# A new order of work for a fused sigmoid-attention and token-mixing kernel on one Trainium2 core

## The chip, the cores and the metric

The kernel runs on one core of one Trainium2 chip. The time is the device time of one execution in microseconds (us); before the change it is 184.6 us, the median of three runs (183.64 to 184.81). The core has five engines with queues of their own, each of which works off its list strictly in order: PE (TensorE, matmuls), DVE (VectorE), ACT (ScalarE), POOL (GpSimd) and SP (SyncE, which here only issues DMAs).

## The reference

Per batch (8) and head (12) the reference computes a sigmoid attention over 448 positions with 64 dimensions, then a token-mixing layer on the joined heads (768 wide):

```python
scores = scale * np.matmul(q, k.transpose(0, 1, 3, 2)) - np.log(S)
attn = 1.0 / (1.0 + np.exp(-scores))
x = np.matmul(attn, v)                  # heads joined: x is (8, 448, 768)
wq = x @ w_q ; wk = x @ w_k             # 64 wide
W_tok = scale * einsum('bsd,btd->bst', wq, wk)
mixed = einsum('bst,btd->bsd', W_tok, x)
out = np.maximum(mixed, 0.0) @ w_out    # float32, (8, 448, 768)
```

## The kernel before, in words

The kernel takes four heads of one batch at a time; such a set is called a *group* here (in the code `quads`), and there are 8 x 3 = 24 of them, numbered 0 to 23. Three groups make a batch (`u`). Matmuls run in bf16 with sums in PSUM, which is used as eight banks, single (`bank1`) or in pairs (`bank2`).

For each group there are these steps, with the line of the instruction in brackets:

- SP loads q, k and v as float32 into a ring of six buffers `ld` (L190, L198). A buffer is free for the sixth load after it when its cast is done.
- The casts to bf16 run on POOL, or on DVE where the table `ORDER` has a dot ahead of the name (L222 for plain casts, L212 for casts that interleave pairs of elements).
- q and k are brought into transposed form in one of four ways, given by letters of the table `PLAN` and recorded in `KIND`: `q`/`k`, by 28 matmuls each on quadrants (64 x 64) of the array (L124), with one copy by DVE for both (L301); `a`/`b`, by 7 matmuls each on the whole array (128 x 128), with one copy each (L280); `c`/`d`, exchanged by POOL (function `arrange`: L167 once, L170 and L173 twice each) and then transposed in blocks by DVE (L272 twice); `r`/`s`/`z`, in quadrants by DVE alone (L265 twice, L252 four times).
- Letter `S` (seven in a group): one slice of scores, four matmuls on quadrants (L121, tiles `banks<-qk`), then the sigmoid on ACT over 896 elements per partition (L332). `T` is an `S` whose sigmoid is put off, so that the next one covers both slices in one instruction of 1792 elements.
- `P` (seven in a group): attention times v, four matmuls on quadrants into one pair of banks; after the seventh the sum is copied to `xt` (L356 on DVE; small `p` on ACT).
- `x`: transposes `xt` to `xn` with 28 matmuls on quadrants into a pair of banks; `X` does it with 7 matmuls on the whole array into a single bank (L124, copy L385).

Once per batch: `W` (six times, x times w_q and w_k), `N` and `U` (tmp, evacuated at L463), `M` (three times, the mixing with its relu, L470), and `O` (the product with w_out, copied at L604 or L651 and stored). POOL copies one half of `wq` for it (L438).

Nothing of this order is left to a scheduler. `PLAN` is a string of letters worked off from left to right, and every step appends its instructions to the lists of the engines. `BANKS` gives the banks in the order of request (digits are pairs, letters single banks). `ORDER` is the order of loads and casts; POOL's casts are appended as soon as their buffers allow it (`pump`), DVE's where `PLAN` has a `1`. `D` issues the next output store. `HELD` and `BEHIND` make some stores and loads wait until a numbered matmul is done.

Of the kernel before, what the change touches and what calls it, by code (L numbers as in the profile page):

```python
# [17 lines left out]
def kernel(  # L18
# [29 lines left out]
    def pool(name, bufs, **kw):  # L48
# [15 lines left out]
    pairs = [banks[:, 2 * n : 2 * n + 2] for n in range(4)]  # L64
    pairs16 = [banks16[:, 2 * n : 2 * n + 2] for n in range(4)]
    BANKS = (
        "abcd0123200233111020302312031203101031021g2012020120h1g21320"
        "132123103103213012302g01h20h1g2031a32102312g12h1201321gh0210"
        "12h01210321g201321g2h01gh201g20132cd302c302302131e301230ef31"
        "0ef3102102c302d320d320123cd20gh120g102310g102hg102312gh10210"  # L70
        "ef130210ef1302120120320312321031021021321a310320321320120123"
        "020210320120c3210210312"
    )
    given = list("".join(BANKS))
    held = set()
# [54 lines left out]
    def xt(u, j):  # L130
# [5 lines left out]


    PLAN = (
        "SSFKESSES1EEqESDD1DESjPPppSpDpPDSSSqS1kSpPPSqSpSkSDPPSPSxSxr"
        "sSWwDDDDSSwzDPpSPppSpPSrSwSwWsSPpXSPNpSpPPSUSqSzMSSkpSpPpSMS"  # L140
        "ppPSSxSxMScPpSdPSpppSSPwWwrWSSXWDWSSosOSNPpPSpppzPSSOOSxSrPP"
        "ppSUSsppzPSoSOSoSoSppMpSPPPPSSWOWWWScSdxWODSMDWSOSxCOSMppScP"
        "DppSPPDSodDoSpxPDPDSCPrPSpDSPOOSNSsSOoDzOOSUSXcSPdpPSSpPPSPo"
        "OWSMSwowWMSSOwWCScpppSxpdpSpPSOoMSPPcDSPPpSpSPOoNSSSdDOoDOOp"
        "xDSPpPxSPpPDSuwcWwdSSMWOoSMSDwwOOSDxpPSPrPSmPpPDooNDSDSosoOz"
        "oSDDSxOOSUDpSDPPPDSPpcDSPoDODSSSodOoOSPMpSPPPSPPSwWwoScMSdOw"
        "wSSWOONSPMPcpSPPPPSSOodXSOSxoSoxSOppSpcUPSPpPSoOSdSxOOSPPPmp"
        "pPSPoSoMmOSOLScllLSLLSDodODSONxOPSpcpdpDPSPSPoOSoSOSOoSUSoSO"
        "SpPPpp1SoSOpSPOSOyppPMpPpplMlmlxlLlxOoONooUoOMmooOmooOoOOOOO"
        "oOOOOooOo"  # L150
    )
    PLAN = "".join(PLAN)
    KIND = ["a"] + [t for t in PLAN if t in "qacr"]
# [364 lines left out]

    opened = []
    stores, o_tiles = [], [0]  # L520
    HELD = {(5, 1, 1): 3040, (5, 2, 0): 3168, (5, 2, 1): 3168}

    def flush(n=None):

# [45 lines left out]
    def out_pair(act, tail):  # L570
# [128 lines left out]
    for _ in range(31):  # L699
# [1 line left out]


    ORDER = (
# [5 lines left out]
    )  # L709
    BEHIND = {("q", 23): (2280, 2280), ("v", 23): (2816, 2530)}  # L710
    BY = {"s": [], "v": []}
    for x in ORDER.split():
        if x[0] == ".":
# [10 lines left out]
    def pump_loads():  # L724
        while len(loaded) < len(ORDER):
            nm, n = ORDER[len(loaded)]
            if len(ring) >= 6 and ring[-6] not in cast:
                break
            emit, m = BEHIND.get((nm, n), (0, 0))
            if emit >= len(products):  # L730
# [204 lines left out]
```

## Time and profile before

| | |
|---|---|
| median of three runs | 184.6 us (183.64 to 184.81) |
| the profiled execution | 184.71 us |
| span from its first to its last instruction | 182.8 us |
| granted TensorE clock, mean | 0.994 |
| busy: PE, DVE, ACT, POOL | 170.4, 134.3, 159.4, 116.8 us |
| DMA moved, mean | 48.51 MB, 265 GB/s |

The profile lists what each engine did in one execution. "Busy" is time in which at least one of its instructions was under way; the instructions of PE and ACT overlap their successors, so the distance from start to start says more of their pace than the duration. Timeline rows give start and duration in us, the engine, the line, the operation, the tiles it writes and reads (out<-in), the shape and the count, and in brackets how long the engine stood idle ahead of it and who ended that. A shape such as `64*64` ahead of a matmul's operands is the part of the array that it uses.

### The profile page before, as it was taken

To read this page: it belongs to the slowest core of one execution; us is meant where nothing else is said; L and a number is where in the kernel's file an instruction comes from. 1 tells how busy PE (TensorE), PEld (TensorE's weight loads), DVE (VectorE), ACT (ScalarE), POOL (GpSimd) and SP (SyncE) were. 2 spreads that over 40 slices of the span, in tenths; PEclk is the share of its full clock that TensorE was granted. 3 is DMA by queue.
4 is the path that set the end of the run, shared out by engine and by line. 5 is a ranking of instruction groups with operands and counts; after the bars stand their busy time and mean duration, and the time that the engine had idled before them with its cause. 6 is when DMAs were issued, how large, how long until landed. Compare 5 with 4: busy or idle time off the path is not lost.

```text
span 182.8 us, 8404 instructions
## 1 busy us (share of the span) xinstructions
PE 170.4 (93%) x3617; PEld 112.8 (62%) x3618; DVE 134.3 (73%) x205; ACT 159.4 (87%) x207; POOL 116.8 (64%) x156
## 2 busy tenths in 40 slices
PE   7887789899999999999999999999999999999980
PEld 7644435545564555565556556556788798899960
DVE  2545699988998898988858887689786885694220
ACT  4699999999999999999998999899989979966230
POOL 1336886999589999699999927999999500000000
PEclk9999999999999999999999999999999999999997
DMA  5999999969999677999999999997589343433775
GB/s 174 371 382 274 329 382 398 364 212 279 351 402 331 219 295 207 353 285 349 396 232 327 349 307 292 359 359 250 193 255 252 106 96 87 95 90 93 176 181 164
DMA packets 24261, 48.51 MB, mean 265 GB/s; under 512 B 3872, under 2 KB 16416, under 8 KB 24224
## 3 DMA queue, kind: packets, MB, share of 16 engines
q1 hardware_dynamic: 24000, 47.69, 79.4%
q8 instruction: 28, 0.46, 1.0%
q10 hardware_dynamic: 224, 0.30, 0.7%
q14 instruction: 9, 0.07, 0.1%
HBM read 35.78 MB, written 11.01 MB: 256 GB/s over the span
## 4 chain that ended last, share of the span: by engine, by line
PE 76%; ACT 12%; DMA 3%; POOL 3%; issue 2%; DVE 1%; POOLq 0%; ACTq 0%
PE banks L121 72%; ACT at L332 12%; PE banks L124 4%; DMA ld<-in_v_dram 3%; POOL v L222 1%; POOL qk L212 1%; POOL qk L173 1%; POOL wout L755 0%; DVE xn L385 0%; ACT qk L806 0%; DVE ld L558 0%; ACT ld L558 0%; DVE zeros L691 0%; DVE zeros L690 0%; POOLq L222 0%
## 5 line engine op out<-in xcount | busy, mean ns | idle before, releaser
L332 ACT ACTIVATE at<-banks 128x896 bf16<-128x896 f32 x168 | 141.1, 943 | 5.4 <-PE banks L121 4.8
L121 PE MATMUL banks<-wout,mx 64*64 64x384 bf16 (+2 forms) x816 | 65.4, 324 | 0.0
L121 PE MATMUL banks<-qk 64*64 64x448 bf16 x672 | 60.7, 360 | 3.8 <-ACT at L332 3.0
L212 POOL CAST qk<-ld 128x896 bf16<-128x896 f32 x38 | 44.7, 1191 | 8.2 <-issue 5.6
L121 PEld LDWEIGHTS <-mx 64*64 64x64 bf16 (+2 forms) x816 | 39.2, 105 | 16.2 <-issue 6.0
L121 PE MATMUL banks<-at,v 64*64 64x448 bf16 x672 | 46.5, 350 | 0.8 <-ACT at L332 0.4
L121 PEld LDWEIGHTS <-qk 64*64 64x64 bf16 x672 | 26.5, 105 | 24.8 <-issue 17.8
L356 DVE CAST xt<-banks 128x896 bf16<-128x896 f32 x23 | 25.0, 1086 | 7.6 <-PE banks L121 5.7
L121 PEld LDWEIGHTS <-v 64*64 64x64 bf16 x672 | 22.9, 106 | 6.8 <-issue 1.7
L470 DVE TENSOR_SCALAR mx<-banks 128x896 bf16<-128x896 f32 (+1 forms) x21 | 19.9, 956 | 4.9 <-PE banks L121 4.2
L222 POOL CAST v<-ld 128x896 bf16<-128x896 f32 x22 | 20.3, 930 | 2.9 <-DMA ld<-in_v_dram 2.7
L272 DVE STREAM_TRANSPOSE qk<-qk 128x448 f32<-128x448 f32 x26 | 16.0, 630 | 0.1
L385 DVE COPY xn<-banks 128x896 bf16<-128x896 bf16 x21 | 13.1, 624 | 3.6 <-PE banks L124 2.6
L252 DVE STREAM_TRANSPOSE qk<-qk 32x448 f32<-32x448 f32 x24 | 15.3, 636 | 0.6
L170 POOL COPY qk<-qk 32x448 uint32<-32x448 uint32 x26 | 14.4, 554 | 1.6
L173 POOL COPY qk<-swap 32x448 uint32<-32x448 uint32 x26 | 14.4, 554 | 1.5
L121 PE MATMUL banks<-xt,wqk 64*64 64x448 bf16 (+1 forms) x84 | 13.8, 353 | 0.2 <-ACT at L332 0.2
L651 DVE COPY o<-banks 128x384 f32<-128x384 f32 x17 | 9.4, 554 | 3.4 <-PE banks L121 3.0
L124 PEld LDWEIGHTS <-xt 64*64 64x64 bf16 (+1 forms) x588 | 9.8, 108 | 3.0 <-issue 1.5
L124 PE MATMUL banks<-ident,xt 64*64 64x64 bf16 (+1 forms) x588 | 10.4, 194 | 0.2
L121 PE MATMUL banks<-wqk,tmp 64*64 64x448 bf16 (+3 forms) x72 | 8.5, 291 | 0.0
L121 PE MATMUL banks<-wq,tmp 64*64 64x448 bf16 (+2 forms) x72 | 8.4, 292 | 0.0
(67 smaller groups left out, 135.3 us busy)
## 6 DMA issues: line engine op xcount, KB each, us to landing
ld<-in_q_dram SPq DMA_DIRECT2D x24, 448.0 KB, 6.2
ld<-in_v_dram SPq DMA_DIRECT2D x24, 448.0 KB, 5.9
ld<-in_k_dram SPq DMA_DIRECT2D x23, 448.0 KB, 5.9
out_dram<-o SPq DMA_DIRECT2D x38, 192.0 KB, 4.7
out_dram<-ld SPq DMA_DIRECT2D x14, 192.0 KB, 2.8
ld<-in_moe_w_out_dram SPq DMA_DIRECT2D x6, 384.0 KB, 4.6
wout<-wout SPq DMA_DIRECT2D x6, 192.0 KB, 6.0
out_dram<-o SPq DMA_DIRECT2D x4, 96.0 KB, 1.9
```

The costliest lines, as they stand in the source:

```text
L121: products.append(nc.tensor.matmul(*args, **kw))
L124: products.append(nc.tensor.transpose(*args, **kw))
L170: eng.tensor_copy(out=w[lo, 1], in_=w[hi, 0])
L173: eng.tensor_copy(out=w[hi, 0], in_=z[lo])
L212: COPY[e](out=f[:, :, "qk".index(nm)].rearrange("p e i d y -> p e y i d"), in_=ld.pop((nm, n)).rearrange("p (y i e d) -> p e y i d", y=2, ...
L222: COPY[e](out=t16.rearrange("p i b d -> p b i d"), in_=ld.pop((nm, n)).rearrange("p b (i d) -> p b i d", i=NI),)
L252: nc.vector.transpose(out=qk[n][other : other + 32, h].rearrange("p t i n -> p (t i n)").bitcast(F32), in_=w[own : own + 32, 1 - h],)
L272: nc.vector.transpose(out=qk[n][:, t].rearrange("p t i n -> p (t i n)").bitcast(F32), in_=w)
L332: nc.scalar.activation(dst, src, ACTF.Sigmoid, bias=attn_bias, scale=attn_scale)
L356: COPY[eng](out=xt(u, j), in_=ps)
L385: COPY[eng](out=xn, in_=ps)
L470: nc.vector.tensor_scalar(dst, ps, moe_scale, 0.0, ALU.mult, ALU.max)
```

## The change

The three tables are replaced; no function changes. `PLAN`, `BANKS` and `ORDER` are new as a whole, and `HELD` and `BEHIND` are empty, so that no load and no store waits for a numbered matmul.

```diff
     PLAN = (
-        "SSFKESSES1EEqESDD1DESjPPppSpDpPDSSSqS1kSpPPSqSpSkSDPPSPSxSxr"
+        "SSFKESSESEEDDEqSkDSSEpSpPPppSPSPPDS1qkS1ppSpSapSbSPTSSDrXSxS"
...
-    HELD = {(5, 1, 1): 3040, (5, 2, 0): 3168, (5, 2, 1): 3168}
+    HELD = {}
...
     ORDER = (
-        ".q1 k1 .v0 .k2 q2 v1 q3 k3 q4 w0 k4 v2 k5 q5 v3 q6 k6 v4 k7 w5 "
-        "q7 v5 w3 q8 w1 k8 w2 w4 w6 v6 v7 q9 k9 k10 v8 q10 q11 v9 v10 "
...
+        "q1 k1 v0 q2 v1 k2 .q3 q4 .k3 k4 w0 v2 q5 k5 q6 v3 q7 k6 v4 k7 v5 "
+        "w6 k8 w5 q8 w1 w3 w4 v6 w2 v7 q9 k9 v9 v10 .q10 k10 .v8 k11 q11 "
...
-    BEHIND = {("q", 23): (2280, 2280), ("v", 23): (2816, 2530)}
+    BEHIND = {}
```

Counted over both programs, the work itself is the same but for the following. Two groups change from 28 matmuls per operand on quadrants to 7 on the whole array (groups 3 and 6), and so do two transposes of `xt`: 6 x 21 = 126 matmuls fewer. Groups 9, 12 and 17 change from DVE's quadrants to POOL's exchange: 16 groups are exchanged now and were 13, three go in quadrants and were six. DVE makes 13 casts instead of 4: seven more at L212, two more at L222. Four sigmoids become two of double length. A few copies out of PSUM change between ACT and DVE (L604: two more on DVE; L385, L463, L651 and L470: one each).

The first place is POOL's list about group 9, whose casts are those into `qk_1133` before and `qk_1017` now; group 10 is `qk_1275` before and `qk_1230` now, and `wq_99` belongs to batch 1. Before:

```order
L212 CAST qk_1133<-ld_103 128x2x2x224
L212 CAST qk_1133<-ld_104 128x2x2x224
L438 COPY wq_99<-wqk_97 64x448
L212 CAST qk_1275<-ld_105 128x2x2x224
L222 CAST v_1278<-ld_100 128x2x7x64
L212 CAST qk_1275<-ld_101 128x2x2x224
L167 COPY swap<-qk_1275 128x448
L170 COPY qk_1275<-qk_1275 32x448 x2
L173 COPY qk_1275<-swap 32x448 x2
```

And now:

```order
L212 CAST qk_1017<-ld_103 128x2x2x224
L212 CAST qk_1017<-ld_104 128x2x2x224
L167 COPY swap<-qk_1017 128x448
L170 COPY qk_1017<-qk_1017 32x448 x2
L173 COPY qk_1017<-swap 32x448 x2
L438 COPY wq_99<-wqk_97 64x448
L222 CAST v_1296<-ld_105 128x2x7x64
L222 CAST v_1299<-ld_100 128x2x7x64
L212 CAST qk_1230<-ld_102 128x2x2x224
L167 COPY swap<-qk_1230 128x448
L170 COPY qk_1230<-qk_1230 32x448 x2
L173 COPY qk_1230<-swap 32x448 x2
```

Group 9 now has an exchange on POOL between its casts and its transposes, two casts of v stand ahead of group 10, and one of group 10's two casts is gone from POOL.

The second place is the same one in DVE's list. Before, from group 9's transposes on (`qk_1133`), to those of group 10 (`qk_1275`):

```order
L265 STREAM_TRANSPOSE qk<-qk_1133 128x448 x2
L463 CAST tmp<-banks 128x384
L252 STREAM_TRANSPOSE qk<-qk_1133 32x448 x4
L356 CAST xt_91<-banks 128x2x7x64
L651 COPY o<-banks 128x384
L470 TENSOR_SCALAR mx<-banks 128x2x448
L356 CAST xt_92<-banks 128x2x7x64
L272 STREAM_TRANSPOSE qk<-qk_1275 128x448 x2
```

And now, with group 9 as `qk_1017` and group 10 as `qk_1230`:

```order
L272 STREAM_TRANSPOSE qk<-qk_1017 128x448
L212 CAST qk_1230<-ld_101 128x2x2x224
L463 CAST tmp<-banks 128x384
L356 CAST xt_91<-banks 128x2x7x64
L272 STREAM_TRANSPOSE qk<-qk_1017 128x448
L222 CAST v_1294<-ld_103 128x2x7x64
L651 COPY o<-banks 128x384 x2
L470 TENSOR_SCALAR mx<-banks 128x2x448
L356 CAST xt_92<-banks 128x2x7x64
L272 STREAM_TRANSPOSE qk<-qk_1230 128x448 x2
```

Six transposes of group 9 have become two, with a cast of group 10's q and the evacuations of `tmp` and `xt` between them.

More of the change, by code (lines that the diff above doesn't have):

```diff
@@ L66 @@
     BANKS = (
[L67 to L72, printed above, removed]
+        "abcd2300122011333230123201203103c0d3013e012g0120201h2013e123"
+        "102g1h02130130213b21302g01h20h1g2031a32102312g102h012301gh02"
+        "1012h01210321h201321gh201gh201320132cd302c302302131e031203e0"
+        "f13ef1032102dc032032d032102cdg02h120g102302g012hg021302gh102"
+        "10ef130213fe13021201023203123120310210213213a103203213201201"
+        "23020120320c2d03110213212"
     )
```

22 lines of the change are left out of this document (11 added, 11 removed), and 6 rows, old and new, of the table ORDER.

## The prediction

> **What bounds the kernel now.** I read the page's busy line and chain first, then busy time by stage, then the engines' rows in order of time.
>
> ```profile
> PE 170.4 (93%) x3617; PEld 112.8 (62%) x3618; DVE 134.3 (73%) x205; ACT 159.4 (87%) x207; POOL 116.8 (64%) x156
> PE 76%; ACT 12%; DMA 3%; POOL 3%; issue 2%; DVE 1%; POOLq 0%; ACTq 0%
> ...
> core 0: us, PE busy (x) PEld busy (x) DVE busy (x) ACT busy (x) POOL busy (x), PEclk, DMA share, GB/s
> 0.00:6.70 6.70, 5.28 (x49) 4.72 (x49) 2.32 (x8) 2.48 (x4) 1.73 (x9) 1.00 0.72 227
> 6.70:52.90 46.20, 40.42 (x942) 22.53 (x943) 36.91 (x54) 45.84 (x57) 33.69 (x39) 1.00 0.96 338
> 52.90:130.00 77.10, 77.10 (x1314) 43.91 (x1306) 64.92 (x97) 73.99 (x98) 67.87 (x89) 1.00 0.90 306
> 130.00:159.30 29.30, 29.30 (x834) 25.14 (x830) 20.77 (x29) 27.78 (x35) 13.53 (x20) 1.00 0.57 156
> 159.30:177.60 18.30, 18.28 (x505) 16.45 (x497) 9.02 (x18) 8.99 (x17) 0.00 (x0) 1.00 0.52 128
> 177.60:182.80 5.20, 0.00 (x0) 0.00 (x0) 0.36 (x1) 0.32 (x1) 0.00 (x0) 0.80 0.62 171
> ```
>
> The stages are cut where the bound changes. From 6.7 to 52.9 us ACT is busy 45.84 of 46.20 us, all with sigmoids (56 end in it), while PE has 5.8 us without any matmul. From 52.9 to 177.6 us PE is never idle. ACT still has 73.99 of 77.10 us there, POOL 67.87, and DMA 0.90 of its engines. So ACT sets the first stage, PE the rest, with ACT and POOL close behind; the last 5.2 us are the last copies and stores, which the change leaves as they are.
>
> A busy PE still loses time. The distances from start to start show where:
>
> ```profile
> 80.55 1.14 PE L121 MATMUL banks<-wout,mx 128*128 128x384 bf16 x6
> 81.52 0.35 PE L121 MATMUL banks<-xt,wqk 128*128 128x448 bf16 x1
> ...
> 86.92 0.37 PE L121 MATMUL banks<-qk 64*64 64x448 bf16 x4
> 87.11 0.56 PE L121 MATMUL banks<-at,v 64*64 64x448 bf16 x8
> 87.49 0.38 PE L121 MATMUL banks<-qk 64*64 64x448 bf16 x4
> 87.80 1.15 PE L121 MATMUL banks<-wout,mx 128*128 128x384 bf16 x6
> 88.88 0.38 PE L121 MATMUL banks<-wqk,tmp 64*64 64x448 bf16 x2
> ```
>
> Four score matmuls followed by others on quadrants take 0.19 us (86.92 to 87.11); the same four followed by whole-array ones take 0.31 (87.49 to 87.80). Six output matmuls followed by whole-array ones take 0.97, followed by quadrants 1.08. So going from one tile size to the other costs PE about 0.12 us, either way. Counted along the program's PE list, the tile size changes 84 times before and 86 times now: some 10 us of each.
>
> **The change part by part.** First PE, in the whole-array transposes:
>
> ```profile
> 77.44 0.38 PE L121 MATMUL banks<-qk 64*64 64x448 bf16 x4
> 77.75 0.56 PE L124 MATMUL banks<-ident,xt 128*128 128x128 bf16 x7
> 78.25 0.38 PE L121 MATMUL banks<-qk 64*64 64x448 bf16 x4
> ...
> 130.33 0.39 PE L124 MATMUL banks<-ident,xt 64*64 64x64 bf16 x28
> 130.55 0.66 PE L121 MATMUL banks<-wout,mx 64*64 64x384 bf16 x12
> ```
>
> 28 transposes on quadrants take 0.22 us; 7 on the whole array, between scores, take 0.50, and the scores ahead of them 0.31 instead of 0.19. So the 126 matmuls fewer are no gain: 0.50 - 0.12 for the way back = 0.38, less 0.22, is 0.16 us more for each of six, 1.0 us, beside the changes of tile size. But all six lie ahead of the 56th sigmoid (two groups early, and four `X` there against two before), where ACT sets the pace: I cost them at nothing. Their cover is the 5.8 us of idle PE there; without it they cost 1.0 us.
>
> The changes of tile size move the same way. Ahead of the 56th sigmoid there are now 29 of them (21 before), behind it 57 (63 before). Values, W, M and O ahead of that sigmoid are the same in number. So PE's work behind 52.9 us differs by six changes of tile size: -6 x 0.12 = **-0.7 us** on the path, and the +8 early ones (1.0 us) go into the same cover.
>
> ACT: its sigmoids and their slices stay; no row shows a sigmoid of 1792 elements, so I bound the two pairs by those of 896. Two single ones start 0.83 us apart (19.11 us for 23, first row below), so a pair costs at most 1.66, and the saving is nothing to a few hundredths. I take nothing.
>
> ```profile
> 39.68 19.11 ACT L332 ACTIVATE at<-banks 128x896 bf16<-128x896 f32 x23
> ...
> L212 POOL CAST qk<-ld 128x896 bf16<-128x896 f32 x38 | 44.7, 1191 | 8.2 <-issue 5.6 <-DMA ld<-in_k_dram 1.0 <-DMA ld<-in_q_dram 0.9
> L222 POOL CAST v<-ld 128x896 bf16<-128x896 f32 x22 | 20.3, 930 | 2.9 <-DMA ld<-in_v_dram 2.7
> L170 POOL COPY qk<-qk 32x448 uint32<-32x448 uint32 x26 | 14.4, 554 | 1.6
> L167 POOL COPY swap<-qk 128x448 uint32<-128x448 uint32 x13 | 7.3, 560 | 0.8
> L252 DVE STREAM_TRANSPOSE qk<-qk 32x448 f32<-32x448 f32 x24 | 15.3, 636 | 0.6
> L265 DVE STREAM_TRANSPOSE qk<-qk 128x448 f32<-128x448 f32 x12 | 7.0, 621 | 0.1
> L272 DVE STREAM_TRANSPOSE qk<-qk 128x448 f32<-128x448 f32 x26 | 16.0, 630 | 0.1
> L222 DVE CAST v<-ld 128x896 bf16<-128x896 f32 x2 | 1.2, 618 | 0.0
> L356 DVE CAST xt<-banks 128x896 bf16<-128x896 f32 x23 | 25.0, 1086 | 7.6 <-PE banks L121 5.7 <-ACT at L332 1.6
> L293 DVE COPY qk<-banks 128x896 bf16<-128x896 bf16 x2 | 1.3, 626 | 1.9 <-PE banks L124 1.9
> L301 DVE COPY qk<-banks 128x1792 bf16<-128x1792 bf16 x3 | 3.3, 1088 | 3.2 <-ACT at L332 2.7 <-PE banks L124 0.5
> ```
>
> POOL: seven L212 casts and two L222 casts go, 7 x 1.19 + 2 x 0.93 = 10.2 us; three exchanges come, each 0.56 + 4 x 0.554 = 2.78, together 8.3. Net -1.9 us of 116.8: no relief to speak of. DVE: three groups lose 4 x 0.636 + 2 x 0.621 and gain 2 x 0.630, together -7.6; four whole-array copies come at 0.626 (the nearest row, L293), two L301 at 1.09 go, +0.3; two L222 casts, +1.2. The seven L212 casts have no DVE row. The ends are 0.62, the plain cast from SBUF, and 1.09, the cast of as many elements at the slow rate (L356, out of PSUM): 4.3 to 7.6 us. I take 0.62, since that row has the same engine, memories and types. Net -1.8 us on DVE, at the other end +1.5; neither is on the path by itself. [...]
>
> Loads and stores: the same bytes. Without the numbered waits, the last loads come earlier and the stores as soon as they are ready; DMA is 0.57 and 0.52 busy where that happens, so it is worth nothing either way.
>
> What stalls is not in these sums. The tightest place is group 9, and there is a new wait:
>
> ```profile
> 51.65 1.20 POOL L212 CAST qk<-ld 128x896 bf16<-128x896 f32 x1 [0.76 <-DMA ld<-in_k_dram]
> 56.77 0.56 POOL L167 COPY swap<-qk 128x448 uint32<-128x448 uint32 x1
> 58.62 1.17 POOL L173 COPY qk<-swap 32x448 uint32<-32x448 uint32 x2
> ...
> 54.80 2.64 DVE L252 STREAM_TRANSPOSE qk<-qk 32x448 f32<-32x448 f32 x4
> 57.47 1.09 DVE L356 CAST xt<-banks 128x896 bf16<-128x896 f32 x1
> ...
> 59.04 3.49 ACT L332 ACTIVATE at<-banks 128x896 bf16<-128x896 f32 x4
> ```
>
> Group 9's second cast waits for its load and ends at 52.85 us. Before, DVE's quadrants follow at once and end at 57.44; the group's first sigmoid starts at 59.04. The order puts the same loads ahead of this one, on DMA engines that are 0.96 busy, so I let it land at the same time. Now an exchange comes between: 56.77 to 59.79, 3.0 us, so it ends at 55.9. DVE's first transpose waits for that, and behind it on DVE stand a cast (0.6 to 1.1), the copy of `tmp` (about 0.6), the copy of `xt` (1.1) and the second transpose (0.63). Their sum with the first is 3.6 to 4.1, so group 9 is ready at 59.5 to 60.0 and its sigmoid at about 59.9 to 60.4 with scores between: 0.8 to 1.3 us late. PE waits meanwhile for the pair of banks that `tmp` still holds. If the load lands 1 us earlier the cost is nearly nothing; between 0 and 1.3 I take **+0.7 us**.
>
> The sum against the profiled execution: 184.71 - 0.7 + 0.7 = 184.7; the median of the runs lies 0.1 under it, so **184.6 us**.
>
> **The rivals.** *Faster: ACT is fed without a gap.* [...] ACT's idle time from 52.9 to 130 us is 3.1 us. If half of it goes and group 9 costs nothing: 184.6 - 0.7 - 1.6 = 182.3. For it: ACT, PE and DVE all have less or equal work there. Against it: PE is busy through all of that stage, and a fed ACT cannot pass it.
>
> *Slower: POOL comes late, and stays late.* From the end of group 9's exchange to the end of group 10's, POOL has a copy (0.56), two casts of v (1.86), one of k (1.19) and 3.0 us of exchange: 6.6 us for seven sigmoids, which ACT does in 5.8. So it falls 0.8 us further behind. If a cast on DVE also holds POOL up for its 0.62 us, the two around group 10 add 1.2, and a group 9 at its upper end 0.6 more than I took: 184.6 + 0.8 + 1.2 + 0.6 = 187.2. It decides from the point where group 9's exchange ends after 56 us. For it: POOL is 88% busy there already (67.87 of 77.10). Against it: one cast of four is taken off POOL here, and five more later on. [...]
>
> *Slower in the first stage: the cover is not there.* If the early whole-array work ends up in front of scores that ACT is waiting for, the 1.0 us of transposes and the 1.0 us of changed tile sizes come on the path: 184.6 + 2.0 = 186.6. Against it: 5.8 us of idle PE.
>
> **How the numbers follow.** About 1%, 1.85 us, is what a measurement of this kernel can tell from no change. My forecast, no change, has 0.48; the fed ACT 0.24; the late POOL 0.23; the missing cover 0.05. So faster 0.24, same 0.48, slower 0.28. The forecast's own range, by group 9 between 0 and +1.3 and the tile-size term between -0.7 and 0, is 183.9 to 185.9. The range reaches to the faster case and to just under the late POOL: 182.3 to 187.0.
>
> **What would show it.** Right: 86 changes of tile size at 0.12 us each, a first stage with ACT above 45 of 46 us and the 56th sigmoid ending within 0.5 us of 52.9, whole-array transposes at 0.5 us, L212 on DVE near 0.62 us, and an idle time of DVE ahead of group 9's first L272 that POOL's L173 ends. Wrong: a 56th sigmoid more than 1 us off; casts of POOL or DVE that grow longer beside each other; L212 on DVE near 1.1 us; or new waits of ACT for PE in groups 10 to 13, which would bring the late POOL. A last matmul ahead of 176 us would show that PE's own losses were not what bounds the middle.

## The result: 192.0 us, four per cent slower

The changed kernel takes 192.0 us (191.5 to 196.1) against 184.1 us (183.6 to 184.8); the ratio is 1.042, with a 95% interval of 1.036 to 1.047. Its profiled execution took 191.5 us, with a span of 189.7 us (182.8 before). The forecast was 184.6 us, no change, in a range of 182.3 to 187.0: wrong, and outside the range.

The page of the changed kernel, in its busy line, the DMA share in 40 slices, and the chain:

```profile
PE 170.9 (90%) x3492; PEld 112.4 (59%) x3492; DVE 131.9 (70%) x204; ACT 159.9 (84%) x203; POOL 118.7 (63%) x163
...
DMA  5999999869998989979979956994079433541686
...
PE 54%; POOL 17%; DMA 15%; issue 4%; DVE 4%; ACT 2%; SPq 1%; POOLq 0%; DVEq 0%; ACTq 0%
```

Each engine's work is what it was within 3 us (PE 170.4 before, ACT 159.4, DVE 134.3, POOL 116.8). The chain is not: PE and ACT held 88% of it, now 56%; POOL and DMA have 32%. And DMA has a slice of 0 in the middle of its busy time. The second and the third stage, from the windows of the changed kernel:

```profile
52.90:130.00 77.10, 73.76 (x1292) 42.00 (x1296) 58.35 (x89) 70.93 (x90) 68.88 (x94) 1.00 0.89 302
130.00:159.30 29.30, 27.23 (x717) 21.67 (x717) 21.60 (x30) 25.03 (x32) 13.99 (x22) 1.00 0.48 149
```

PE was never idle behind 52.9 us; now it stands still for 3.3 us of the second stage and 2.1 of the third. The timeline has the places (start, length, engine, operation, and in brackets the idle time before it and what ended it):

```profile
15.40 0.57 PE L121 MATMUL banks<-at,v 64*64 64x448 bf16 x8 [1.21 <-POOL v L222]
...
56.29 0.65 DVE L272 STREAM_TRANSPOSE qk<-qk 128x448 f32<-128x448 f32 x1 [2.14 <-POOL qk L173]
56.86 0.63 DVE L212 CAST qk<-ld 128x896 bf16<-128x896 f32 x1
57.39 0.53 DVE L463 CAST tmp<-banks 128x384 bf16<-128x384 f32 x1
57.97 0.65 PE L121 MATMUL banks<-wout,mx 128*128 128x384 bf16 x3 [1.68 <-DVE tmp L463]
...
81.02 0.72 DVE L212 CAST qk<-ld 128x896 bf16<-128x896 f32 x1 [2.38 <-DMA ld<-in_q_dram]
82.23 0.84 PE L121 MATMUL banks<-qk 64*64 64x448 bf16 x4 [0.94 <-DVE o L651]
...
146.21 1.40 POOL L212 CAST qk<-ld 128x896 bf16<-128x896 f32 x1 [3.98 <-DMA ld<-in_q_dram]
148.23 0.28 PE L121 MATMUL banks<-wqk,tmp 64*64 64x224 bf16 x2 [1.90 <-issue]
```

Each time something stands in the order of an engine ahead of data that is not there; at 56 and 81 us the copies out of PSUM that PE needs stand behind it. At 15.4 us it is PE itself, with the values of group 1 ahead of v. At 56.3 it is DVE, for POOL's exchange of group 9. At 81.0 it is the cast of q of group 14, on DVE, for its load. At 146 POOL waits for q of group 23, and at 148 PE for nothing that the profile shows. The wait at 15.4 us is no steady cost of the change: k22_later below is the same program up to there and has nothing of it (its row in the table), so it comes and goes with the execution.

What these loads themselves waited for stands in the timelines of POOL, SP and DVE, first for q of group 14, then for v of group 22 and those behind it:

```profile
75.22 0.93 POOL L222 CAST v<-ld 128x896 bf16<-128x896 f32 x1
76.17 0.93 SPq L190 DMA_DIRECT2D ld<-in_q_dram  x1
...
122.87 4.41 SPq L657 DMA_DIRECT2D out_dram<-o  x6
...
136.44 0.68 DVE L212 CAST qk<-ld 128x896 bf16<-128x896 f32 x1
...
137.14 0.39 SPq L198 DMA_DIRECT2D ld<-in_v_dram  x1
137.62 1.72 SPq L190 DMA_DIRECT2D ld<-in_k_dram  x1
...
139.91 0.42 SPq L190 DMA_DIRECT2D ld<-in_q_dram  x1
```

Six buffers go round, and a load is issued when the cast six loads earlier is done. For q of group 14 that is POOL's cast of v of group 12: it ends at 76.15 us, SP issues the load at 76.17, and it lands at 80.90, where DVE has been waiting for 2.38 us. For v of group 22 it is the cast of k of group 22, one of the thirteen on DVE, which stands near the 140th sigmoid: it ends at 137.12, the load is issued at 137.14, and nothing at all is issued from 127 to 137 us. And so along the whole trace: of the loads issued behind 55 us, eleven in the changed kernel land only 0.05 to 0.32 us ahead of the start of their cast, in the kernel before none less than 0.75 us ahead (both worked out from the times of landing in the traces).

In the table below the same is counted by the starts of the sigmoids, each stretch less the same stretch of the kernel before (us, worked out from the ACT rows of the traces; "end" is from the last sigmoid to the end of the span). The other rows belong to the experiments.

| traced run | to 24th | to 56th | to 64th | to 88th | to 136th | to 152nd | to 168th | end |
|---|---|---|---|---|---|---|---|---|
| changed kernel | +1.3 | 0.0 | +1.2 | +2.3 | -0.6 | +3.4 | +0.1 | -0.7 |
| k22_later | -0.2 | +0.4 | +1.1 | +6.0 | -0.6 | +0.6 | +0.1 | +0.2 |
| q14_on_pool | +1.3 | -0.2 | +0.5 | +1.0 | +1.6 | +5.9 | +0.1 | -0.7 |
| g9_behind_tmp | +2.5 | -0.2 | +0.9 | +5.1 | -0.6 | +2.4 | +0.1 | -0.7 |
| eight_buffers | +0.5 | -0.2 | -0.3 | +1.0 | 0.0 | +0.6 | +0.1 | -0.7 |
| seven_buffers | 0.0 | -0.3 | -0.4 | +1.0 | 0.0 | +1.5 | +0.1 | -0.7 |
| order_six_buffers | +0.1 | -0.2 | +0.3 | +1.8 | +4.7 | +1.3 | +0.1 | -0.7 |
| order_eight_buffers | +2.2 | -0.2 | +0.2 | +0.9 | -0.5 | +4.7 | +0.1 | -0.7 |
| before_exchange3 | -0.5 | +0.3 | +2.1 | +1.0 | +0.9 | +0.5 | 0.0 | -0.6 |
| before_dve_casts | 0.0 | +0.3 | 0.0 | +2.4 | +2.5 | 0.0 | 0.0 | -0.8 |
| before_whole8 | +0.5 | -0.1 | 0.0 | +0.8 | +1.4 | 0.0 | 0.0 | +0.4 |
| eight_buffers_g9_quadrants | -0.3 | -0.2 | +0.7 | +0.9 | -0.1 | +0.6 | +0.1 | -0.7 |
| before_eight_buffers | +0.4 | +0.1 | 0.0 | 0.0 | +0.1 | 0.0 | 0.0 | -0.9 |
| before_nothing_held | +0.5 | -0.1 | 0.0 | 0.0 | 0.0 | +0.5 | 0.0 | -0.1 |
| before_dve_casts_eight | +1.6 | -0.2 | 0.0 | +3.2 | +0.6 | 0.0 | 0.0 | +0.4 |
| before_quadrants_eight | +2.6 | -0.1 | -0.1 | 0.0 | 0.0 | +1.0 | 0.0 | -0.8 |

The ratios leave out executions more than 1.5% above the fastest of their kernel, medians and ranges do not; the traced ones of g9_behind_tmp, q14_on_pool and order_eight_buffers are such slow executions, that of seven_buffers is the fastest of its six.

### The profile page after: what moved, and what is told of

Same layout as the page of the kernel before. It is cut to its first block, busy times and chain, and to the rows that moved or that the text cites. A ratio compares the mean times of both kernels' runs of the same rounds, so it can differ in the third digit from the quotient of the medians.

```text
span 189.7 us, 8174 instructions
## 1 busy us (share of the span) xinstructions
PE 170.9 (90%) x3492; PEld 112.4 (59%) x3492; DVE 131.9 (70%) x204; ACT 159.9 (84%) x203; POOL 118.7 (63%) x163
## 4 chain that ended last, share of the span: by engine, by line
PE 54%; POOL 17%; DMA 15%; issue 4%; DVE 4%; ACT 2%; SPq 1%; POOLq 0%; DVEq 0%; ACTq 0%
PE banks L121 51%; DMA ld<-in_k_dram 8%; POOL qk L212 6%; PE banks L124 3%; POOL qk L173 3%; POOL v L222 3%; DMA ld<-in_moe_w_out_dram 3%; DMA ld<-in_q_dram 2%; POOL qk L170 2%; DMA ld<-in_v_dram 2%; ACT at L332 2%; POOL swap L167 1%; POOL wout L755 1%; DVE xt L356 1%; POOL k L222 1%
## 5 line engine op out<-in xcount | busy, mean ns | idle before, releaser
L121 PE MATMUL banks<-qk 64*64 64x448 bf16 x672 | 61.8, 358 | 5.9 <-ACT at L332 2.4
L212 POOL CAST qk<-ld 128x896 bf16<-128x896 f32 x31 | 37.0, 1211 | 8.7 <-DMA ld<-in_q_dram 6.5
L470 DVE TENSOR_SCALAR mx<-banks 128x896 bf16<-128x896 f32 (+1 forms) x22 | 21.0, 960 | 8.0 <-PE banks L121 7.8
L272 DVE STREAM_TRANSPOSE qk<-qk 128x448 f32<-128x448 f32 x32 | 19.9, 631 | 5.6 <-POOL qk L173 5.6
L222 POOL CAST v<-ld 128x896 bf16<-128x896 f32 x20 | 19.3, 970 | 6.0 <-DMA ld<-in_v_dram 3.0
L170 POOL COPY qk<-qk 32x448 uint32<-32x448 uint32 x32 | 17.7, 555 | 1.9
L173 POOL COPY qk<-swap 32x448 uint32<-32x448 uint32 x32 | 17.7, 554 | 1.9
L385 DVE COPY xn<-banks 128x896 bf16<-128x896 bf16 x20 | 12.3, 616 | 4.4 <-PE banks L124 3.4
L167 POOL COPY swap<-qk 128x448 uint32<-128x448 uint32 x16 | 9.8, 611 | 3.7 <-DVE qk L212 2.8
L651 DVE COPY o<-banks 128x384 f32<-128x384 f32 x16 | 8.6, 547 | 1.5 <-PE banks L121 1.1
## 6 DMA issues: line engine op xcount, KB each, us to landing
out_dram<-o SPq DMA_DIRECT2D x38, 192.0 KB, 5.0
out_dram<-ld SPq DMA_DIRECT2D x14, 192.0 KB, 2.9
wout<-wout SPq DMA_DIRECT2D x6, 192.0 KB, 7.2
```

The source lines that it names most:

```text
L121: products.append(nc.tensor.matmul(*args, **kw))
L167: eng.tensor_copy(out=z, in_=w[:, 1])
L170: eng.tensor_copy(out=w[lo, 1], in_=w[hi, 0])
L173: eng.tensor_copy(out=w[hi, 0], in_=z[lo])
L212: COPY[e](out=f[:, :, "qk".index(nm)].rearrange("p e i d y -> p e y i d"), in_=ld.pop((nm, n)).rearrange("p (y i e d) -> p e y i d", y=2, ...
L222: COPY[e](out=t16.rearrange("p i b d -> p b i d"), in_=ld.pop((nm, n)).rearrange("p b (i d) -> p b i d", i=NI),)
```

## The experiments

The first theory: the work is right in the sums, and what is lost are four separate stalls, made by the order in which casts and loads stand. The rivals: the thirteen casts on DVE cost as such, by their work; the three exchanges instead of quadrants do it, whatever the order; the whole-array transposes and changes of tile size do it; the numbered waits that went.

### One place at a time

**k22_later** moves one load:

```diff
-        "k17 q17 v16 .q19 k18 v17 v18 q18 k19 v19 v20 k20 .k22 q20 q21 "
-        "k21 v21 q22 v22 .k23 .v23 q23 "
+        "k17 q17 v16 .q19 k18 v17 v18 q18 k19 v19 v20 k20 q20 q21 "
+        "k21 v21 q22 .k22 v22 .k23 .v23 q23 "
```

> The changed kernel with one load moved: k of group 22 stands behind q of group 22 in the load order instead of ahead of q of group 20; its cast stays on DVE at the same place. Theory (a cast that is placed late holds a load buffer, and with it SP's queue): the hole in SP's issues from 126.6 to 137.1 us goes, so do the pile-up of loads and stores behind it, POOL's 3.98 us wait for q of group 23 and PE's 1.90 us wait at 148.2: 192.0 - 2.7 = 189.3 us (188.5 to 190.0). [...] Rival 2 (PE's wait at 148 us is its own, whatever DMA does): the hole goes and the wait stays, 191.5 or more.

**g9_behind_tmp** moves group 9's first transpose (`c`) behind the step that ends in the copy of tmp (`U`):

```diff
-    ...CDDOSxcSpP1PPSUSPpPd1S...
+    ...CDDOSxSpP1PPSUcSPpPd1S...
```

> The changed kernel with one step moved: the first transpose of group 9 on DVE stands behind the copy of tmp instead of ahead of it. POOL's exchange stays as it is. Theory (the order of DVE's queue costs the time: a PSUM copy stands behind a transpose that waits): DVE's wait is shorter by the cast and the copy that now fill it, PE's 1.68 us wait for tmp near 58.0 us is gone and the first sigmoid of group 9 comes about 1.2 us sooner: 192.0 - 1.2 = 190.8 us (190.3 to 191.3). Rival (the exchange on POOL ends too late, whatever stands in DVE's queue): the sigmoid is as late as now, 192.0 within 0.3.

**q14_on_pool** takes the dot off q of group 14 and its `1` out of the order:

```diff
-        "k12 q12 v12 k13 .q13 v14 .v11 k14 .q14 .v13 v15 q15 .k16 k15 q16 "
+        "k12 q12 v12 k13 .q13 v14 .v11 k14 q14 .v13 v15 q15 .k16 k15 q16 "
```

> The changed kernel with one of its thirteen DVE casts back on POOL, that of q of group 14. Theory (the cast stands in DVE's queue ahead of its data: 2.38 us of waiting for the load at 81.0 us, with copies out of PSUM behind it): this wait goes, about 1.0 us: 191.0 us (190.4 to 191.4). Rival 1 (all thirteen casts cost alike, by their work on DVE): 7.3 us over thirteen, a part of 0.6 at most: 191.4 to 192.0. Rival 2 (POOL comes late): its 1.2 us more on POOL make groups 14 and 15 later: 192.0 to 193.2.

Measured: 192.2 us for k22_later (190.4 to 193.1; ratio 1.043, 1.037 to 1.049), 191.8 for g9_behind_tmp (191.1 to 194.1; 1.041, 1.035 to 1.047), 192.3 for q14_on_pool (189.9 to 194.2; 1.034, 1.028 to 1.040). The forecasts of k22_later and g9_behind_tmp missed by time. q14_on_pool is open: by its ratio it is 0.8% (some 1.4 us) under the changed kernel, near the 1.0 us of its forecast, but the two intervals overlap. In the traces each edit does what the theory said at its own place: k22_later loses 0.6 us instead of 3.4 from the 136th to the 152nd sigmoid, q14_on_pool has no wait for q of group 14 at 81 us, and in g9_behind_tmp PE waits 0.80 us for tmp instead of 1.68. But in these executions the time is lost elsewhere. In k22_later's timeline the same cast of q of group 14 waits longer:

```profile
81.12 1.48 DVE L212 CAST qk<-ld 128x896 bf16<-128x896 f32 x1 [3.72 <-DMA ld<-in_q_dram]
...
83.09 0.84 PE L121 MATMUL banks<-qk 64*64 64x448 bf16 x4 [3.04 <-DVE o L651]
```

The load lands at 81.00 us there, as late as in the changed kernel (80.90), though all that leads up to it came about 1 us sooner. Of the 6.0 us in its row some 1.7 are a stretch at half clock behind this pause: from 84.03 to 87.44 us the granted clock was 0.50 (last section), and half of 3.41 us is 1.7, an estimate.

In q14_on_pool, which has that cast on POOL, the next cast in DVE's order, v of group 13, waits in its place:

```profile
82.92 1.12 DVE L222 CAST v<-ld 128x896 bf16<-128x896 f32 x1 [1.47 <-DMA ld<-in_v_dram]
...
84.62 0.38 PE L121 MATMUL banks<-qk 64*64 64x448 bf16 x4 [1.76 <-DVE xn L385]
```

And in g9_behind_tmp the cast on DVE that now comes first waits for its own load, with tmp behind it:

```profile
56.85 0.68 DVE L212 CAST qk<-ld 128x896 bf16<-128x896 f32 x1 [1.69 <-DMA ld<-in_q_dram]
57.41 0.56 DVE L463 CAST tmp<-banks 128x384 bf16<-128x384 f32 x1
...
58.02 0.65 PE L121 MATMUL banks<-wout,mx 128*128 128x384 bf16 x3 [0.80 <-DVE tmp L463]
```

So the four places are not four separate causes. In all three traces it is a load that comes late. That the change is a sum of independent stalls fell here with k22_later and g9_behind_tmp.

### The price of the whole-array transposes

**before_whole8** turns eight `x` of the kernel before into `X` (and their pairs of banks into single ones):

```diff
-    ...WWWScSdxWODSMD...
+    ...WWWScSdXWODSMD...
```

> The kernel before with eight of its transposes of x between the 62nd and the 136th sigmoid made on the whole array (seven matmuls instead of 28; ten more changes of tile size). Prediction's steps 0.16 us more for each transpose and 0.12 us for each change of tile size, on PE where it is the bound: 8 x 0.16 + 10 x 0.12 = 2.5 us, 187.1 us (186.3 to 187.6). Rival (matmuls are what PE's time goes by: 168 fewer are no loss, and a change of tile size costs nothing of its own): 184.6 or under.

Measured: 187.4 us (185.9 to 188.7), ratio 1.016 (1.011 to 1.022): the prediction's prices, and not the rival. In the trace the eight take 2.2 us between the 64th and the 136th sigmoid, 2.5 expected for eight transposes and ten changes of tile size together; the run does not tell the two prices apart. PE's own row of work shows it, 172.2 us against 170.4 with 168 matmuls fewer and no new wait behind the first sigmoids:

```profile
PE 172.2 (93%) x3449; PEld 112.3 (60%) x3450; DVE 134.5 (72%) x205; ACT 160.0 (86%) x207; POOL 117.1 (63%) x156
```

### The loads, all at once

**eight_buffers** (the changed kernel) and **before_eight_buffers** (the kernel before) get two more load buffers and nothing else; **eight_buffers_g9_quadrants** has group 9 back in quadrants as well (`c` to `r`, `d` to `s` and `z`):

```diff
-    lds = [singles.tile([P, 2 * NI * HD], F32, name=f"ld{n}") for n in range(6)]
+    lds = [singles.tile([P, 2 * NI * HD], F32, name=f"ld{n}") for n in range(8)]
...
-        return lds[(nld[0] - 1) % 6]
+        return lds[(nld[0] - 1) % 8]
...
-            if len(ring) >= 6 and ring[-6] not in cast:
+            if len(ring) >= 8 and ring[-8] not in cast:
```

> The changed kernel with eight load buffers instead of six, nothing else: the same casts on the same engines in the same order. Theory (the order of the casts no longer fits a ring of six: a load is issued when the cast six before it in the load order is done, and where that is 3 to 7 sigmoids ahead of its own cast, 4 to 6 us from issue to landing come too late): DVE's wait for q of group 14 near 81 us goes and with it the 1.3 us lost there, the hole in SP's issues from 126.6 to 137.1 us goes, and with the pile-up behind it the 2.7 us lost at 148 us: 192.0 - 4.0 = 188.0 us (187.0 to 189.0). What is lost by 20 us and at group 9 stays. [...] Rival 2 (PE's waits for nothing that the profile shows are its own): the hole goes, a wait of PE for issue of 1 us or more stays somewhere behind 75 us, and the time is 190 or more.

> The kernel before with eight load buffers instead of six. Theory: there the sixth cast ahead is done 6 sigmoids or more before each cast, so nothing waits for a buffer that PE or ACT wait for in turn: 184.0 us, within 0.8. Rival (more buffers are worth something to any order, so that what they bring the changed kernel says nothing of its order): 182.5 or less.

> The changed kernel with eight load buffers and with group 9 back in quadrants on DVE, as before (no exchange on POOL for it). Theory: beside what eight buffers bring (188.0), DVE no longer waits for POOL ahead of the cast of tmp, and the 1.2 us lost at group 9 are back: 186.8 us (186.0 to 187.8), with no wait of PE for tmp above 0.5 us near 57 us. Rival (the quadrants' 3.8 us of DVE cost as much as the wait): no better than eight buffers alone, 188.0 or more.

**before_exchange3** is the kernel before with groups 9, 12 and 17 exchanged (`r`, `s`, `z` to `c`, `d`).

> The kernel before with groups 9, 12 and 17 exchanged by POOL instead of taken in quadrants by DVE, nothing else: before's order, casts and loads. Prediction's step (group 9's exchange between POOL's last cast and DVE's transposes): 0 to 1.3 us, taken at 0.7, so 184.7 us (184.0 to 185.3). Rival (the exchange makes POOL late from there on, in groups 10 to 13): 186 or more. Rival (the exchanges are hidden in an order that is not the changed kernel's): 184.0 within 0.3.

Measured: eight_buffers 184.7 us, ratio to the kernel before 0.998 (0.995 to 1.002); before_eight_buffers 185.4 us, 1.001 (0.997 to 1.004); eight_buffers_g9_quadrants 186.2 us, 1.006 (1.003 to 1.009); before_exchange3 187.6 us, 1.012 (1.007 to 1.016).

Two buffers take all of the 4% away, more than the 4.0 us expected. They bring the kernel before nothing, so they are not worth something to every order. The thirteen casts are still on DVE, the three exchanges still on POOL, the whole-array transposes still there, so none of these costs as such what was lost. The chain of eight_buffers, its stages, what PE waits for (total, times, longest), the first transpose of group 9 in the timeline, and the group of its DVE casts:

```profile
PE 64%; ACT 14%; POOL 8%; issue 4%; DMA 3%; DVE 3%; SPq 0%; ACTq 0%; POOLq 0%; DVEq 0%
...
52.90:130.00 77.10, 75.84 (x1319) 43.84 (x1309) 61.60 (x93) 73.14 (x94) 70.72 (x98) 1.00 0.89 299
130.00:159.30 29.30, 29.30 (x795) 23.54 (x797) 21.82 (x30) 27.55 (x34) 9.19 (x14) 1.00 0.47 136
...
PE banks L121 <- DVE tmp L463: 0.2, 1, 0.2
...
53.74 0.65 DVE L272 STREAM_TRANSPOSE qk<-qk 128x448 f32<-128x448 f32 x1 [0.60 <-POOL qk L173]
...
L212 DVE CAST qk<-ld 128x896 bf16<-128x896 f32 x7 | 5.7, 818 | 0.0
```

The chain is PE and ACT again, DMA is 3% of it instead of 15%, and the last row is the point: the seven casts of q and k on DVE waited 2.4 us for a load in the changed kernel and wait for none now. At group 9 DVE waits 0.60 us for the exchange instead of 2.14, since the loads are sooner there: k of group 9 lands at 49.35 us instead of 51.94. Taking the quadrants back brings nothing (1.006 against 0.998). Not all is gone: 1.0 us is still lost from the 64th to the 88th sigmoid and 0.6 behind the 136th, and 0.7 less at the end makes up for part of it. That end is not the work of more buffers, as two expectations below have it: the changed kernel has the same -0.7 with six. One part was expected wrongly. SP still has a hole, between its row at 119.02 us (4.71 long) and that at 133.35:

```profile
119.02 4.71 SPq L657 DMA_DIRECT2D out_dram<-o  x6
133.35 0.39 SPq L198 DMA_DIRECT2D ld<-in_v_dram  x1
133.83 0.42 SPq L190 DMA_DIRECT2D ld<-in_q_dram  x1
```

But only two loads are left behind it instead of four, and q of group 23 is issued 6 us sooner. So the hole by itself was not what cost the time.

In before_exchange3 the exchange in the place of quadrants does cost, with six buffers and without any cast on DVE. Its waits, and in its timeline POOL's last cast of group 9:

```profile
DVE qk L272 <- POOL qk L173: 6.8, 4, 3.0
...
PE banks L121 <- DVE tmp L463: 2.1, 1, 2.1
...
51.48 1.20 POOL L212 CAST qk<-ld 128x896 bf16<-128x896 f32 x1 [1.10 <-DMA ld<-in_k_dram]
```

2.1 us at group 9, 1.0 at group 12, 0.9 behind it; the prediction had 1.3 at the upper end for group 9. The load is not later than before: the cast starts at 51.48 us, at 51.65 before. So in this order the exchange alone costs PE more than the prediction allowed.

### Is it the order of the loads, or where the casts stand?

Counted along the program from the 45th sigmoid on, the changed kernel has ten loads that are issued less than 7 sigmoids ahead of the place of their cast, the kernel before two, the changed kernel with eight buffers two. **order_six_buffers** changes the order of loads from the 36th on, so that by that count no load from there on has less than 8; **order_eight_buffers** has this order, eight buffers and the transpose of x near the 137th sigmoid on quadrants, which makes three edits in one.

```diff
-        "w6 k8 w5 q8 w1 w3 w4 v6 w2 v7 q9 k9 v9 v10 .q10 k10 .v8 k11 q11 "
-        "k12 q12 v12 k13 .q13 v14 .v11 k14 .q14 .v13 v15 q15 .k16 k15 q16 "
-        "k17 q17 v16 .q19 k18 v17 v18 q18 k19 v19 v20 k20 .k22 q20 q21 "
-        "k21 v21 q22 v22 .k23 .v23 q23 "
+        "w6 k8 w5 q8 w1 w3 w4 v6 w2 v7 q9 k9 .q10 k10 v9 .v8 q11 k11 q12 "
+        "k12 v10 k13 k14 .q13 .v11 .q14 v12 .v13 q15 k15 q16 v14 v15 k17 "
+        "q17 .k16 k18 v16 q18 k19 v17 .q19 k20 v18 q20 q21 v19 k21 q22 v20 "
+        "q23 .k22 v21 .k23 v22 .v23 "
```

> The changed kernel with six load buffers as it has, and another order of loads and of POOL's casts from the 36th load on: such that every load is issued 8 sigmoids or more ahead of the place of its cast (casts of v moved later, the thirteen casts on DVE where they are). Theory (order and ring don't fit each other): this brings back what eight buffers brought, less the 0.7 us that they save by output buffers behind the last sigmoid: 184.7 + 0.7 = 185.4 us (184.4 to 186.6), no hole in SP's issues above 6 us, no wait of DVE for a load above 1 us behind 50 us. Rival (eight buffers help by more transfers in flight, in any order): 189.5 or more. Rival (POOL's later casts of v come late for the values): waits of PE for v, 187 or more.

> The changed kernel with both, the other load order and eight buffers, and with its whole-array transpose of x near the 137th sigmoid on quadrants. Theory: the loads no longer bound anything; from eight buffers' 184.7 us the transpose takes 0.16 + 2 x 0.12 = 0.4 us, the last stalls near 80 and 148 us 0.5 each where they were loads: 183.5 us (182.6 to 184.7). Rival (PE's own work bounds it now, and both kernels have the same): 184.7 within 0.4.

**before_nothing_held** empties the two tables of numbered waits of the kernel before (`HELD`, `BEHIND`).

> The kernel before without its numbered waits: neither the last two loads nor three stores wait for a given matmul. Prediction's step: nothing, 184.4 us within 0.6. Rival (the waits keep the last loads out of the stores' way, and without them PE waits in the last third as the changed kernel does at 148 us): 186 or more, lost behind the 136th sigmoid.

Measured: order_six_buffers 191.8 us (ratio 1.033, 1.027 to 1.039), order_eight_buffers 189.2 us (1.021, 1.015 to 1.026), before_nothing_held 185.9 us (1.004, 1.001 to 1.007). The last lies between the prediction's step and its rival: a ratio of 1.0035, unrounded, is some 0.6 us, and the trace loses 0.5 us where the rival had it, behind the 136th sigmoid. The first two are misses. In order_six_buffers the hole and the wait at 148 us are gone, and others have come (the timeline):

```profile
72.34 0.38 PE L121 MATMUL banks<-at,v 64*64 64x448 bf16 x4 [1.38 <-POOL v L222]
...
96.45 0.67 DVE L212 CAST qk<-ld 128x896 bf16<-128x896 f32 x1 [2.27 <-DMA ld<-in_k_dram]
...
98.15 0.57 PE L121 MATMUL banks<-qk 64*64 64x448 bf16 x8 [1.62 <-DVE xt L356]
```

The first row is the rival that was named: the casts of v, moved later on POOL, come late for the values. The second is a load that is late although the count gives it 8 sigmoids: the count runs along the program, and a buffer comes free when POOL has really got to the cast. So a distance counted in steps is no distance in time. Whether some order would do with six buffers stays open.

order_eight_buffers loses most of its time in its trace at one pause that comes with its third edit: PE stands still for 2.73 us up to 133.81 us, for DVE's copy of xn (L385), and a stretch at half clock follows (granted clock 0.50 from 135.12 to 138.53 us). On quadrants x takes a pair of banks, `BANKS` asks for one of the same two banks next, for the output product, and that has to wait until xn is copied. So this run does not say what order and buffers do together.

### The casts alone, and one buffer at a time

**before_dve_casts** puts ten casts of the kernel before on DVE (a dot in the load order and a `1` in the order of steps for each, at the lead that the changed kernel gives them); **before_dve_casts_eight** has eight buffers as well. **seven_buffers** is the changed kernel with seven; **before_quadrants_eight** is the kernel before with eight and its two late `X` as `x`.

```diff
-        "q7 v5 w3 q8 w1 k8 w2 w4 w6 v6 v7 q9 k9 k10 v8 q10 q11 v9 v10 "
+        "q7 v5 w3 q8 w1 k8 w2 w4 w6 v6 v7 q9 k9 k10 .v8 .q10 q11 v9 v10 "
```

> The kernel before, six buffers, with ten of its casts (q of 10, 13, 14 and 19, k of 16, 22 and 23, v of 8, 11 and 13) moved from POOL to DVE, at the lead over their use that the changed kernel gives them; loads and all else as before. Theory (a cast put later on another queue gives its buffer back later, and with six buffers the loads behind it come late): 187 us (185.8 to 190), with waits of DVE or POOL for loads that the kernel before does not have. [...] Rival (they cost nothing, and the loads' own order is what matters): 184.5 within 0.6.

> The same with eight load buffers. Theory: the loads are in time again, 184.5 us (183.6 to 185.3). [...] What it does worse than the kernel before is the price of the casts on DVE themselves.

> The changed kernel with seven load buffers. Theory (lateness of loads, a matter of degree): part of the 7 us comes back, the wait at 81 us shrinks by about the 1 to 2 us that one cast earlier gives: 188 us (186 to 190). Rival (eight buffers helped by something else, such as more room for the last outputs): at most the 0.7 us of the end, 191.0 or more.

> The kernel before with eight buffers and its two whole-array transposes of x behind the 60th sigmoid on quadrants. Theory (0.16 us for each and 0.12 us for each of two changes of tile size fewer, on PE where it is the bound, and 0.8 us behind the last sigmoid by two more buffers for outputs): 184.0 - 0.6 - 0.8 = 182.6 us (182.0 to 183.8). Rival (what PE saves is waited for elsewhere): 184.0 within 0.4.

Measured: before_dve_casts 189.8 us (ratio 1.024, 1.017 to 1.031) and with eight buffers 189.4 us (1.023, 1.018 to 1.029). By the times the theory fails here: in that order ten casts on DVE cost 4 to 5 us, with six buffers and with eight. The timeline of before_dve_casts shows how:

```profile
58.28 0.68 DVE L212 CAST qk<-ld 128x896 bf16<-128x896 f32 x1
58.85 1.07 DVE L356 CAST xt<-banks 128x896 bf16<-128x896 f32 x1
...
59.09 0.56 POOL L167 COPY swap<-qk 128x448 uint32<-128x448 uint32 x1 [5.87 <-DVE qk L212]
...
59.98 0.57 PE L121 MATMUL banks<-at,v 64*64 64x448 bf16 x8 [1.02 <-DVE xt L356]
```

Here the load is there. The cast waits for nothing, it just stands ahead of the copy of xt for which PE waits, and POOL's exchange needs its result and stands idle for 5.9 us. Of the three longest waits of PE behind the 56th sigmoid two are of this kind (1.02 and 1.04 us). The third is the theory's: PE waits 1.75 us at 87.15 us, behind a cast of v on DVE that waits 1.59 us for its load. With eight buffers DVE waits for no load any more, but PE waits 1.79 us at 78.46 for a copy of xt that stands behind two casts. So a cast on DVE has a price that its place sets: 1 to 2 us ahead of a copy out of PSUM that PE waits for. In the changed kernel with eight buffers the thirteen stand elsewhere, and the kernel as a whole is no slower than the one before.

seven_buffers takes 187.9 us (185.8 to 189.2; ratio 1.014, 1.007 to 1.020), between six and eight: a matter of degree, as the theory has it. before_quadrants_eight takes 185.8 us (1.007, 1.004 to 1.010) where 182.6 was expected. Its two transposes bring 0.0 us before the 88th sigmoid and lose 1.0 behind the 136th. There PE waits 0.98 us at 132.58 for a copy of `o`: the pair of banks that x now takes has one bank that is still in use. So the 0.6 us that the two should bring stayed untested. The rest of this execution's loss is a wait in the first stage, in its timeline:

```profile
21.94 0.25 PE L124 MATMUL banks<-ident,k 64*64 64x64 bf16 x7 [2.41 <-issue]
```

No version that was run is faster than the kernel before.

## Why the prediction was wrong

**The step that failed is "Loads and stores: the same bytes", with its end "so it is worth nothing either way".** It looked at bytes and at the numbered waits, and took the times of the loads as given. But a load's time is not set by its bytes or by its place in the list alone; it is set by the cast that frees its buffer, six loads earlier (the load of q of group 14 was issued 0.02 us behind that cast), and the change moves casts in the order and from queue to queue. The prediction followed what each cast costs and never which load waits for it. Of the 7.0 us between the two traced executions 3.4 lie behind the hole at 127 to 137 us and 2.3 around the late q of group 14; with eight buffers it is 0.6 and 1.0. Two more buffers, and no other edit, take the ratio from 1.042 to 0.998. The numbered waits, the other half of this step, are worth some 0.6 us.

The same trust in a load did no harm where the prediction spelled it out, at group 9 ("I let it land at the same time"). Its k lands at 51.94 us, 51.60 before, and POOL ends the two casts of the group at 53.18, where the prediction had 52.85:

```profile
50.89 2.29 POOL L212 CAST qk<-ld 128x896 bf16<-128x896 f32 x2
```

**The sums of the work were about right, and that the total comes out to 0.1 us is luck.** eight_buffers has the change's whole work and runs at the time of the kernel before (184.7 us, forecast 184.6), and each of its engines is busy as long as before within 1.3 us. But its trace has losses and gains that the prediction does not have (+1.0, +0.6 and, at the end, -0.7 us), and its group 9 costs nothing (-0.3 in the table). PE has 1.3 us of idle time left in the second stage and none in the third, so PE bounds the rest, as the prediction said.

**Tile size and whole-array transposes:** 0.12 and 0.16 us, together, hold where they are added (2.2 us in the trace, 2.5 expected). Where two transposes were taken back, a wait for a bank took the place. **The cover:** with eight buffers the 56th sigmoid starts 0.2 us later than before, so the early whole-array work is covered, as costed. In the changed kernel it is 1.3 us later, through the wait for v of group 1 at 15.4 us, which k22_later does not have; this is not the rival with the missing cover, which was about PE's own work.

**DVE and POOL:** the cast of q and k on DVE was taken at 0.62 us and takes 0.665 in the mean, near the lower end (0.818 in eight_buffers, where one of the seven takes 1.69). POOL's sum was taken 1.9 us lower and is 1.9 higher. These groups of the changed kernel show how:

```profile
L212 POOL CAST qk<-ld 128x896 bf16<-128x896 f32 x31 | 37.0, 1211 | 8.7 <-DMA ld<-in_q_dram 6.5 <-DMA ld<-in_k_dram 1.7
...
L222 POOL CAST v<-ld 128x896 bf16<-128x896 f32 x20 | 19.3, 970 | 6.0 <-DMA ld<-in_v_dram 3.0 <-PE banks L124 1.6 <-PE banks L121 0.6
...
L167 POOL COPY swap<-qk 128x448 uint32<-128x448 uint32 x16 | 9.8, 611 | 3.7 <-DVE qk L212 2.8
...
L212 DVE CAST qk<-ld 128x896 bf16<-128x896 f32 x7 | 4.7, 665 | 2.4 <-DMA ld<-in_q_dram 2.4
```

Casts and copies of POOL are longer than before in the mean (1211 against 1191, 970 against 930, 611 against 560 ns): 31 x 0.02 + 20 x 0.04 + 16 x 0.05 = 2.2 of these 3.8 us. It sits in the few that run beside a cast on DVE. The 26 of POOL's casts at L212 that overlap none take 1193 ns in the mean, as before; of the five that do, two take 1402 and 1580. The 13 copies at L167 without one take 561 ns, the three with one 792 to 858. One cast of v on DVE, beside POOL, takes 1.37 us instead of 0.62. So in some of these overlaps the two engines hold each other up, POOL by 0.2 to 0.4 us at a time. No run shows the 0.62 us per cast that the sum to 187.2 takes for it. This hold-up is no part of what was lost, since eight_buffers has it too (a POOL cast at L212 of 1.59 us at 79.92, a DVE cast of v of 1.36 us at 56.85).

**Group 9:** the mechanism was as told, DVE's first L272 waits for POOL's L173 and PE for the pair of banks of tmp. Its size is +1.2 us, 0.5 above the 0.7 that was taken and inside 0 to 1.3, and 2.1 in before_exchange3. **The rival "POOL comes late, and stays late"** was on the right side, but had 2.6 us (187.2) where 7.4 came (192.0), and for the most part POOL was not late by its own work: its L212 waited 8.2 us for loads (1.9 before), and with eight buffers it has as much work (118.0 us) and holds 8% of the chain instead of 17. What is left of the rival is the 1.0 us from the 64th to the 88th sigmoid in eight_buffers: the chain runs through POOL from 55 to 72 us there, and DVE waits 1.08 us for its L173. **The rival "ACT is fed without a gap"** did not come, and no run shows the 1.6 us that its sum takes off: from 52.9 to 130 us ACT was idle for 6.2 us in the changed kernel (70.93 busy of 77.10) and for 4.0 with eight buffers (73.14), against 3.1 before.

**What could have been seen:** in the timeline of before neither POOL nor DVE waits for a load for more than 0.3 us behind 55 us. That says only that the old order fits six buffers. The list of loads with the cast that frees each buffer would have shown ten loads of the new order with a lead of 0 to 6 sigmoids, six of them with at most one, where the old has two, with 3 and 6. In the page of the changed kernel a load takes 5.7 to 6.2 us from issue to landing (medians of q, k and v), and seven sigmoids take 5.8. As order_six_buffers shows, a good count alone would not have been enough.

## What to carry to other kernels

Where loads go through a small ring of buffers, a cast or copy that is moved later, or to a queue that gets to it later, delays the load that stands a ring's length behind it; write down for each load the instruction that frees its buffer, and the time between. Distances counted along the program are not enough, since an in-order engine gets there late: 8 sigmoids of distance still left a wait of 2.27 us for a load in order_six_buffers. When stalls jump from place to place as they are mended one by one, look for what they share: here two more buffers told more than any reordering.

## What the runs showed of the hardware

**Behind some pauses of PE its granted clock was 0.50.** The stretch of k22_later around its wait at 83 us (the last but two columns is the granted clock):

```profile
80.62:84.03 3.41, 0.85 (x35) 0.58 (x35) 2.91 (x5) 0.52 (x2) 2.64 (x5) 1.00 0.88 305
84.03:87.44 3.41, 3.41 (x49) 2.01 (x40) 2.25 (x5) 1.82 (x2) 1.99 (x4) 0.50 0.91 295
```

PE was busy for 0.85 us of the first stretch, and the second ran at half clock. It was the same in order_eight_buffers, and with a shorter pause in order_six_buffers:

```profile
131.70:135.12 3.42, 1.30 (x14) 0.65 (x17) 2.06 (x3) 0.67 (x2) 2.54 (x3) 1.00 0.91 337
135.12:138.53 3.41, 3.41 (x72) 2.16 (x68) 1.21 (x2) 2.20 (x4) 0.09 (x1) 0.50 0.52 142
...
95.35:98.76 3.41, 1.79 (x31) 0.85 (x30) 2.31 (x4) 2.42 (x5) 1.38 (x3) 1.00 0.99 341
98.76:102.18 3.42, 3.42 (x12) 1.47 (x11) 1.78 (x4) 1.54 (x2) 3.24 (x5) 0.50 0.69 197
```

In g9_behind_tmp nothing follows, though PE stood for 3.05 us up to 85.71:

```profile
80.79:84.20 3.41, 1.87 (x41) 1.10 (x40) 0.39 (x1) 2.72 (x4) 3.22 (x5) 1.00 0.83 299
84.20:87.61 3.41, 1.81 (x53) 1.31 (x56) 3.41 (x7) 0.92 (x1) 2.57 (x5) 1.00 0.90 316
87.61:91.03 3.42, 3.42 (x45) 1.77 (x38) 3.04 (x6) 3.25 (x4) 3.30 (x5) 1.00 0.93 284
```

Nor in the changed kernel behind its wait at 58 us, with PE busy for 1.72 us of 3.41:

```profile
55.53:58.94 3.41, 1.72 (x23) 0.77 (x16) 2.65 (x5) 1.95 (x3) 3.23 (x5) 1.00 0.92 270
58.94:62.35 3.41, 3.36 (x41) 1.76 (x44) 3.38 (x5) 3.30 (x4) 3.23 (x5) 1.00 0.91 287
```

Which pauses are followed by half clock these rows do not settle: 1.79 us of work in order_six_buffers were, 1.72 us in the changed kernel were not. By an estimate from the rows a stretch of 3.41 us at 0.50 costs up to 1.7 us of PE's work, beside the pause ahead of it. That fits the wide spread of kernels with pauses of 1.5 to 3 us (189.9 to 194.2 us in q14_on_pool), but as each has one trace, it is argued, not shown; one should not read a single time of theirs.

**Two pauses of PE had no engine late.** The changed kernel's 1.90 us at 148.2 us and before_quadrants_eight's 2.41 us at 21.9 us end with "issue". In both, loads (and at 148 us stores) had just been issued in a row. The page of the changed kernel has a DMA queue that it calls "instruction", with a share of the same 16 engines:

```profile
q8 instruction: 27, 0.44, 0.9%
```

These are 27 packets of 16 KB, beside 6984 matmuls and weight loads in that trace; before it is 28 beside 7235. In both pauses one of them was under way: it ended at 146.96 and at 20.38 us, and PE went on 1.3 and 1.6 us later. Whether PE waited for it no run shows.
